# Windowed attention and two MLPs in fp32 on one core: scores on quarters of the array, PSUM banks shared out anew, weight splits moved and joined

## The chip, the cores and the metric

The kernel runs on one core of a Trainium2 chip. The metric is the device time of one execution in microseconds; "before" was measured in three runs. A profile of one execution gives, for each engine, when every instruction began and what it waited for. PE is TensorE's matmul stream and PEld its weight loads, DVE is VectorE, ACT is ScalarE, POOL is GpSimd, SP is SyncE, which issues nearly all DMAs.

## The reference, cut to what matters

```python
# q, k, v: (batch 4, heads 8, seq 576, head_dim 64)
scores = scale * np.matmul(q, k.transpose(0, 1, 3, 2))
mask = (rel >= 0) & (rel < 64)               # rel = query position - key position
attn = softmax(np.where(mask, scores, -1e9)) # with +1e-9 under the division
x = np.matmul(attn, v)                       # laid out as (2304 tokens, 512)
x = square(relu(x @ w_in1)) @ w_out1         # (512, 2048), (2048, 512)
x = elu(x @ w_in2) @ w_out2                  # the same sizes
```

The weights come as 64-bit floats, the rest as fp32.

## The kernel before

**Numbers.** Attention multiplies plain fp32. Everything after it multiplies a high part and a low part of each operand (`split`: ACT makes the high part by a copy, DVE subtracts it from the original), three products in place of one (`mm3`, L468; `prod`, L686; `prod2`, L884). A 64-bit weight is turned into fp32 words by `decode64` (ACT into `top`, DVE into `y`) before it is split.

**Attention.** The 2,304 tokens are cut into blocks of 512, 256, 512, 512 and 512 (t = 0 to 4), and heads go in pairs (p = 0 to 3), so there are 20 units. `u_S` forms the scores (L380). Since a query sees 64 keys back, a group of 64 queries needs 128 keys. The tile `qd` holds, for each group, the queries of both heads of the pair, each head in its own 64 rows and its own 64 columns, and zeros elsewhere; one 128x128 matmul with contraction over 128 rows then gives 64 queries of both heads against 128 keys. A block of 512 takes eight such matmuls, four to a PSUM bank. Of each 128x128 piece DVE adds the mask and takes the maximum, ACT the exponential and the sum; then DVE divides, one instruction for each piece (ACT does it in block 1). `u_T` transposes (L421), `u_PV` multiplies by V (L434): two matmuls for each group, one for each head, which use 64 columns of the array each (128 rows by 64 columns).

**First MLP.** `m_h` (L468, PSUM tile `ph`) and `m_out` (L468, PSUM tiles `o`) run over blocks 0 to 2, with the attention of later blocks between them. Blocks 3 and 4 go together by a scheme with seven products in place of eight (`stepw`, `prod`, L686, with `outw`); its weights are sums and differences of weight quarters, written to DRAM once (`wd0`) and loaded back (`w0_load`, L706).

**Second MLP.** Its weights take the same form: the generator `portions` decodes, sums, splits and stores them (`put`, L243; tensors `wd1`, `wd2` in DRAM), a step at each `slot()` in the main program. There are 16 tasks of seven quarter matrices, so 112 quarters of 256 KB. The second MLP reads the activations back from DRAM (`x2d`, written by `leave1`, L512) into tiles `xq` (`x_read`, L630), makes its operands `xo` of them (`x_make`) and loads weights as `wr` (`unit_load`, L610). The tiles `xq` take over memory in which `leave1` held block 3's outputs, so they come after those stores.

**What sets the order.** A scheduler lays out every engine's instructions before the run; each engine, SP with its DMAs included, then works through its list in order. All vector and scalar instructions go through one helper, so their line is L54: tiles tell them apart.

Of the kernel before, what the change touches and what calls it, by code (L numbers as in the profile page):

```python
# [26 lines left out]
def window_attention_then_two_mlps(  # L27
# [61 lines left out]
    ps_a = pool(ctx, "ps_a", 2, space=PSUM)  # L89
    ps_h = pool(ctx, "ps_h", 2, space=PSUM)  # L90
# [10 lines left out]
    def zero_q(x, eng):  # L101
        for r in range(2):
            eng.memset(x[r * D:(r + 1) * D, :, 1 - r, :], 0.0)

    def zeros():
        for x in qd:
            zero_q(x, vec)

    def constants():
# [11 lines left out]
        nc.gpsimd.memset(mask[1][:, 0:WIN], NEG)  # L121
# [48 lines left out]
    def decode64(y, z, x):  # L170
# [4 lines left out]
        )  # L175
        vec.scalar_tensor_tensor(
            out=y, in0=x.rearrange("p f w -> p (f w)").bitcast(U32).rearrange("p (f w) -> p f w", w=2)[:, :, 0],
            scalar=13, in1=z, op0=ALU.logical_shift_right, op1=ALU.bitwise_or,
        )

    def w_split(u):
# [8 lines left out]
        if LA <= u < LA + 2:  # L190
            for k, (j, i) in enumerate(UNITS[u]):
# [43 lines left out]
    def put(i, p, k, x):  # L235
        o = small([P, 2, HW], "wo")
        if i == 1:
            z = o.rearrange("p y (m a j) -> p y a m j", m=FT, j=TB)
            split(z[:, 0], z[:, 1], x.rearrange("p (a m j) -> p a m j", m=FT, j=TB), vec)
        else:  # L240
            split(o[:, 0], o[:, 1], x, vec)
        d = wd2[k][:, p] if i == 1 else (wd1 if i == 0 else wd0)[p][:, ORD1.index(k)]
        nc.sync.dma_start(out=d, in_=o.bitcast(F32))  # L243
# [903 lines left out]
```

## Time and profile before

| | us |
|---|---|
| median of three runs (lowest, highest) | 851.28 (850.07, 852.8) |
| the profiled execution, and the span that its trace shows | 852.89, 851.1 |
| PE busy in the span | 819.2 (96%) |
| PEld busy | 747.1 (88%) |
| DVE busy, ACT busy | 590.2 (69%), 579.2 (68%) |
| DMA: bytes moved, mean rate | 214.86 MB, 252 GB/s |

A matmul's duration in the trace is longer than its share of the engine, since matmuls overlap: what a matmul costs is the distance from its start to the next start. One fp32 matmul of the attention leaves two records on PE; a product of high and low parts and a transpose leave one.

### The profile page before, as it was taken

What the parts mean: (1) busy time and instruction counts of PE and PEld (TensorE: products, weight loads), DVE (VectorE), ACT (ScalarE), POOL (GpSimd) and SP (SyncE); (2) the same over time, 40 slices, a digit from 0 to 9 for tenths busy, and PEclk for the clock granted to TensorE, in tenths of its full rate; (3) what the DMA queues carried; (4) which work ended last, traced back from release to release, by engine and by line L of the source; (5) the groups of instructions that cost most, each with busy time, mean ns of one, the idle gap of its engine ahead of it and who ended that gap; (6) DMA issues with size and microseconds to landing.
All of it is one profiled execution on the core that took longest, in us unless ns stands there. A gap on an engine that the chain in (4) does not pass through costs nothing.

```text
span 851.1 us, 14626 instructions
## 1 busy us (share of the span) xinstructions
PE 819.2 (96%) x4908; PEld 747.1 (88%) x4908; DVE 590.2 (69%) x1505; ACT 579.2 (68%) x1353; POOL 5.5 (1%) x21
## 2 busy tenths in 40 slices
PE   6799999999999999999999399999999999999998
PEld 5578889998888888888878299999999999999998
DVE  7777416978466777666667456688767799576875
ACT  6899547787677678867765357766577666477652
POOL 2000000000000000000000000000000000000000
PEclk9999999999999999999999699999999999999999
DMA  9997224657266479999789768788987886877842
GB/s 302 371 400 267 89 76 139 199 191 226 84 230 196 155 236 392 362 345 341 266 287 378 247 230 306 278 304 259 276 294 283 300 261 217 276 266 273 308 131 56
DMA packets 120715, 214.86 MB, mean 252 GB/s; under 512 B 46144, under 2 KB 75328, under 8 KB 112192
## 3 DMA queue, kind: packets, MB, share of 16 engines
q1 hardware_dynamic: 119808, 213.73, 73.0%
q8 instruction: 39, 0.64, 0.3%
q14 instruction: 36, 0.29, 0.1%
q10 hardware_dynamic: 832, 0.20, 0.1%
HBM read 160.41 MB, written 53.48 MB: 251 GB/s over the span
## 4 chain that ended last, share of the span: by engine, by line
PE 85%; DMA 5%; DVE 4%; ACT 4%; issue 1%; SPq 0%; ACTq 0%; DVEq 0%
PE o L468 20%; PE po L884 20%; PE px L686 14%; PE ph L468 11%; PE py L686 10%; PE po L686 6%; PE pa L380 2%; DMA wd<-tl 2%; DVE pb L54 1%; PE pa L434 1%; DMA top<-in_moe_w_out_dram 1%; PE pa L421 1%; DVE y L54 1%; PE px L884 1%; ACT top L54 1%
## 5 line engine op out<-in xcount | busy, mean ns | idle before, releaser
L468 PE MATMUL o<-gs,w 128*128 128x512 f32 (+1 forms) x960 | 217.1, 373 | 0.3 <-ACT ev L54 0.3
L468 PEld LDWEIGHTS o<-gs,w 128*128 128x128 f32 x960 | 167.7, 190 | 30.2 <-ACT ev L54 1.1
L884 PE MATMUL po<-g,wr 128*128 128x384 f32 (+1 forms) x972 | 168.6, 333 | 0.0
L884 PEld LDWEIGHTS po<-g,wr 128*128 128x128 f32 x972 | 167.5, 188 | 0.0
L468 PE MATMUL ph<-xs,w 128*128 128x512 f32 (+1 forms) x576 | 130.0, 366 | 5.6 <-ACT xs L54 3.0
L54 ACT ACTIVATE g<-gr 128x384 fp32r<-128x384 f32 x168 | 86.9, 523 | 56.2 <-PE po L884 49.8
L468 PEld LDWEIGHTS ph<-xs,w 128*128 128x128 f32 x576 | 97.1, 193 | 21.7 <-ACT xs L54 4.0
L54 DVE TENSOR_TENSOR g<-gr,g 128x384 fp32r<-128x384 f32 x168 | 89.9, 551 | 16.1 <-ACT g L54 15.1
L686 PE MATMUL px<-xo,wr 128*128 128x384 f32 x432 | 85.3, 338 | 11.8 <-ACT xo L54 11.5
L686 PEld LDWEIGHTS px<-xo,wr 128*128 128x128 f32 x432 | 76.5, 190 | 12.8 <-ACT xo L54 11.9
L54 DVE TENSOR_TENSOR gs<-g,gs 128x512 fp32r<-128x512 f32 (+1 forms) x64 | 39.8, 623 | 48.1 <-ACT gs L54 47.3
L54 ACT ACTIVATE sy<-px 128x384 f32<-128x384 f32 x69 | 33.8, 490 | 42.2 <-PE px L686 41.7
L54 ACT ACTIVATE pb<-pb,nm 128x128 f32<-128x128 f32 x144 | 55.8, 390 | 9.1 <-DVE nm L54 9.0
L686 PE MATMUL py<-xo,wr 128*128 128x384 f32 x288 | 57.2, 339 | 1.3 <-ACT xo L54 0.7
L686 PE MATMUL po<-xo,wr 128*128 128x384 f32 x288 | 56.2, 334 | 0.0
L686 PEld LDWEIGHTS py<-xo,wr 128*128 128x128 f32 x288 | 51.2, 190 | 2.2 <-ACT xo L54 1.2
L54 DVE TENSOR_TENSOR gr<-gr 128x384 f32<-128x384 f32 x96 | 52.1, 552 | 0.5
L54 DVE TENSOR_TENSOR gr<-sy,py 128x384 f32<-128x384 f32 x48 | 26.6, 554 | 35.7 <-PE py L686 23.3
L686 PEld LDWEIGHTS po<-xo,wr 128*128 128x128 f32 x288 | 50.5, 188 | 0.0
L686 PE MATMUL px<-xo,w 128*128 128x512 f32 x192 | 46.5, 389 | 0.0
L54 ACT ACTIVATE g<-ph 128x512 f32<-128x512 f32 (+1 forms) x48 | 24.7, 517 | 29.0 <-PE ph L468 28.8
L686 PEld LDWEIGHTS px<-xo,w 128*128 128x128 f32 x192 | 36.0, 188 | 7.5
(91 smaller groups left out, 1139.5 us busy)
## 6 DMA issues: line engine op xcount, KB each, us to landing
wr<-wd SPq DMA_DIRECT2D x66, 1024.0 KB, 6.4
wr<-wd SPq DMA_DIRECT2D x24, 768.0 KB, 5.3
wd<-tl SPq DMA_DIRECT2D x56, 256.0 KB, 4.1
w<-wd SPq DMA_DIRECT2D x56, 256.0 KB, 4.8
wd<-wo SPq DMA_DIRECT2D x56, 256.0 KB, 4.9
vr<-in_v_dram SPq DMA_DIRECT2D x16, 512.0 KB, 5.2
wd<-xs SPq DMA_DIRECT2D x32, 256.0 KB, 2.6
wraw<-in_moe_w_in_dram SPq DMA_DIRECT2D x16, 511.8 KB, 8.2
```

Of the source, the lines that this page charges most:

```text
L54: r = fn(*a, **kw)
L380: nc.tensor.matmul(out=ps[:, i * P:(i + 1) * P], lhsT=qr[:, b0 + i].rearrange("p a x -> p (a x)"), rhs=kr[:, o:o + P], start=True, stop=True,)
L421: nc.tensor.transpose(out=ps[:, i:i + P], in_=pb[:, i:i + P], identity=ident)
L434: nc.tensor.matmul(out=ps[d, b * WIN:(b + 1) * WIN], lhsT=vr[:, b % 2, b // 2, d], rhs=pt[:, d], start=True, stop=True,)
L468: last["pe"] = nc.tensor.matmul(out=ps, lhsT=a[x], rhs=b[y], start=(first and i == 0), stop=(final and i == 2))
L686: last["pe"] = nc.tensor.matmul(out=ps[:, :NH], lhsT=w[:, wr_, c * P:(c + 1) * P], rhs=x[:, xr_, c], start=first and n == 0, stop=final an ...
L884: last["pe"] = nc.tensor.matmul(out=ps[m][:, lo:hi], lhsT=w[:, y, m * P:(m + 1) * P], rhs=s[:, x, lo:hi], start=k in fresh and p == 0 and ...
```

## The change

It has five parts.

1. **Scores on quarters.** `q` is loaded as it is, by one DMA, without zeros. A matmul now takes 64 rows of one head (`qr[d, ...]`) and 64 queries: a quarter of the array. Four of them (two heads, two groups of 64 queries) do what two matmuls did. Each head has a PSUM bank of its own; a 128x128 piece now holds two groups of one head.
2. **PSUM.** The pools for `ph` and `pa` (two banks each) give way to four banks handed out by `among`: `ph` has two in block 0 and one afterwards; the attention has two, and three from block 1 on.
3. **One division a bank.** One DVE instruction over 512 columns, with the reciprocals broadcast, replaces four, in block 1 too.
4. **High parts of the first MLP's weights on DVE** (`split_v`), not on ACT.
5. **Second layer's parts two at a time.** `put` takes two quarters where they lie side by side, with one split (two in `wd2`) and mostly one DMA; `stage` replaces `small` and hands out buffers of two quarters; the order in `wd1` and `wd2` fits that. The slots are as many as before.

```diff
--- before.py
+++ after.py
@@ -86,25 +86,14 @@
...
     wts = pool(ctx, "wts", 1)
-    ps_a = pool(ctx, "ps_a", 2, space=PSUM)
-    ps_h = pool(ctx, "ps_h", 2, space=PSUM)
     ps_o = pool(ctx, "ps_o", 1, space=PSUM)
...
-    mask = [cst.tile([P, P], F32, name=f"mask{i}") for i in range(2)]
-    qd = [at.tile([P, 2 * NQ, 2, D], F32, tag=f"qd{i}", name=f"qd{i}", bufs=1) for i in range(2)]
+    mask = [cst.tile([P, P], F32, name=f"mask{i}") for i in range(3)]
...
+    def split_v(hi, lo, x):
+        vec.tensor_copy(hi, x)
+        vec.tensor_tensor(out=lo, in0=x, in1=hi.bitcast(F32), op=ALU.subtract)
...
-                split(w[:, 0], w[:, 1], yf[:, k], vec)
+                split_v(w[:, 0], w[:, 1], yf[:, k])
...
-        split(w[:, :, 0, :], w[:, :, 1, :], yf, vec)
+        split_v(w[:, :, 0, :], w[:, :, 1, :], yf)
...
-    ORD1 = ["a11", "a12", "s2", "s1", "s3", "a22", "s4"]
+    ORD1 = ["a11", "a12", "s2", "s1", "s4", "s3", "a22"]
...
+    ORDK = [1, 2, 5, 6, 7, 4, 3]
...
-    wd2 = {n: drp.tile([P, NP, 2, HW], F32, name=f"wd2_{n}") for n in ORD2}
+    wd2 = drp.tile([P, 7, NP, 2, HW], F32, name="wd2")
...
     def put(i, p, k, x):
-        o = small([P, 2, HW], "wo")
+
...
+        m = x.shape[1]
+        hi, lo, o = stage(m)
...
+            d = wd2[:, ORDK.index(k):ORDK.index(k) + m, p]
         else:
...
-        nc.sync.dma_start(out=d, in_=o.bitcast(F32))
...
+            split(hi, lo, x, vec)
+            d = (wd1 if i == 0 else wd0)[p][:, ORD1.index(k):ORD1.index(k) + m]
+        if o is None:
+            for r, z in enumerate((hi, lo)):
+                nc.sync.dma_start(out=d[:, :, r], in_=z.bitcast(F32))
+        else:
+            nc.sync.dma_start(out=d, in_=o.bitcast(F32))
...
+        left, right = yf[:, :, :HW], yf[:, :, HW:]
+
+        def sums(p, i):
+            sub2(q21, q21, q22, ALU.add)
+            sub2(q11, q21, q11)
+            put(i, p, "s2", left)
+            yield
+            sub2(right, right, yf[:, 0:1, :HW].broadcast_to([P, 2, HW]))
+            put(i, p, "s4", right)
+            yield
...
-            sub2(q21, q21, q22, ALU.add)
-            put(2, p, "s1", q21)
-            sub2(q11, q21, q11)
-            put(2, p, "s2", q11)
-            yield
-            sub2(q12, q12, q11)
-            put(2, p, "s4", q12)
-            sub2(q22, q22, q11)
-            put(2, p, "s3", q22)
-            yield
+            yield from sums(p, 2)
...
-                put(i, p, 1, q11)
-                put(i, p, 2, q21)
-                put(i, p, 3, q22)
+                put(i, p, 1, left)
+                put(i, p, 3, yf[:, 1:2, HW:])
                 yield
                 sub2(q12, q12, q11)
-                put(i, p, 5, q12)
                 sub2(q22, q22, q12)
-                put(i, p, 6, q22)
+                put(i, p, 5, right)
                 yield
                 sub2(q11, q22, q11)
-                put(i, p, 7, q11)
                 sub2(q21, q21, q22)
-                put(i, p, 4, q21)
+                put(i, p, 7, left)
...
-                qr = sc.tile([P, 2 * NQ, 2, D], F32, tag="gs", name="qd", bufs=GB)
-                zero_q(qr, nc.gpsimd)
+                qr = sc.tile([P, NMAX], F32, tag="gs", name="qd", bufs=GB)
             else:
...
-                qr = qd[p % 2]
+                qr = at.tile([P, NMAX], F32, tag="qd", name="qd", bufs=2)
...
-            for a in range(2):
...
-                nc.sync.dma_start(
-                    out=qr[w, :2 * m, a, :],
-                    in_=q[p, w, t0:t0 + n].rearrange("d (b x) -> d b x", x=WIN),
-                )
+            nc.sync.dma_start(out=qr[:, :n], in_=q[p, :, t0:t0 + n])
...
     def u_S(u, alloc):
...
         qr, kr = raw[u]["q"], raw[u]["k"]
+        m = BLOCKS[t] // P
...
-        for b0, m in banks(t):
-            ps = alloc()
-            for i in range(m):
-                o = (b0 + i) * WIN
-                nc.tensor.matmul(
-                    out=ps[:, i * P:(i + 1) * P],
-                    lhsT=qr[:, b0 + i].rearrange("p a x -> p (a x)"), rhs=kr[:, o:o + P],
-                    start=True, stop=True,
-                )
+        pss = [alloc() for _ in range(2)]
+        for i in range(m):
+            for a in range(2):
+                d = slice(a * D, (a + 1) * D)
+                for c in range(2):
+                    o = (2 * i + c) * WIN
+                    nc.tensor.matmul(
+                        out=pss[a][c * WIN:(c + 1) * WIN, i * P:(i + 1) * P],
+                        lhsT=qr[d, o:o + WIN], rhs=kr[d, o:o + P], start=True, stop=True,
+                    )
+        prb[u] = []
...
             pb = at.tile([P, 4 * P], F32, tag="pb", name="pb", bufs=4)
...
                 vec.tensor_tensor_reduce(
-                    out=pb[:, c], in0=ps[:, c], in1=mask[(T0[t] + b * WIN) % S == 0],
+                    out=pb[:, c], in0=pss[a][:, z], in1=mask[1 + lead.index(True) if any(lead) else 0],
...
-            r = rc[:, b0:b0 + m]
...
+            r = rc[:, b0:b0 + w]
...
             vec.reciprocal(out=r, in_=r)
...
-            for i in range(m):
-                c, b = slice(i * P, (i + 1) * P), b0 + i
-                if t == 1:
...
-                    act.activation(
...
-                    )
...
-                    continue
-                last["dve"] = vec.tensor_scalar(
-                    out=pb[:, c], in0=pb[:, c], scalar1=rc[:, b:b + 1], scalar2=None, op0=ALU.mult
-                )
-            prb[u, b0] = pb
...
+            last["dve"] = vec.tensor_tensor(
+                out=x, in0=x, in1=r.unsqueeze(2).broadcast_to([P, w, P]), op=ALU.mult
+            )
+            prb[u].append((pb, w))
...
-        for b0, m in banks(u[0]):
-            pb = prb.pop((u, b0))
+        for pb, w in prb.pop(u):
...
-        for b, pt in enumerate(pts):
+        m = BLOCKS[t] // P
+        for b in range(2 * m):
             for a in range(2):
...
-                    out=ps[d, b * WIN:(b + 1) * WIN],
-                    lhsT=vr[:, b % 2, b // 2, d], rhs=pt[:, d], start=True, stop=True,
+                    out=ps[d, b * WIN:(b + 1) * WIN], lhsT=vr[:, b % 2, b // 2, d],
+                    rhs=pts[a * m + b // 2][:, (b % 2) * WIN:(b % 2 + 1) * WIN], start=True, stop=True,
...
-        ps = ps_h.tile([P, 512], F32, tag="h", name="ph")
+        ps = h_alloc(t)
...
-    a_alloc = lambda: ps_a.tile([P, 512], F32, tag="a", name="pa")
...
+    def spot(k, name):
+        return ps_o.tile([P, 512], F32, tag=f"b{k}", name=name)
...
+    def among(ks, name):
+        turns[ks] = turns.get(ks, -1) + 1
+        return spot(ks[turns[ks] % len(ks)], name)
+
+    def h_alloc(t):
+        return among((0, 1) if t == 0 else (0,), "ph")
+
+    def a_alloc():
+        return among((1, 2, 3) if late[0] else (2, 3), "pa")
...
-    def small(shape, name):
-        turn[1] += 1
-        if la:
-            return la[0].tile(shape, F32R, tag=f"gs{turn[1] % 4}", name=name, bufs=1)
-        if lw and turn[1] % 6 < 4:
-            return lw[0].tile(shape, F32R, tag="wo", name=name, bufs=4)
-        if hw:
-            return half(2 + turn[1] % 2)
-        return xs[1, turn[1] % KD][:, :, HW:]
...
+    def stage(m):
+
+        n = turn[1] = turn[1] + 1
+        if lw or hw:
+            if n % 3 == 0 and hw:
+                o = hw[1].rearrange("p y f -> p (y f)").rearrange("p (k y f) -> p k y f", k=2, y=2)
+            elif lw:
+                o = lw[0].tile([P, 2, 2, HW], F32R, tag="wo", name="wo", bufs=2)
+            else:
+                o = at.tile([P, 2, 2, HW], F32R, tag="wo", name="wo", bufs=1)
+            o = o[:, :m]
+            return o[:, :, 0], o[:, :, 1], o
+        if n % 3 == 0:
+            o = at.tile([P, 2, 2, HW], F32R, tag="wo", name="wo", bufs=1)[:, :m]
+            return o[:, :, 0], o[:, :, 1], o
+        k = 2 * (n % 3) - 2
+        return *(xs[1, (k + r) % KD][:, :m, HW:] for r in range(2)), None
...
-        src = wd1[p] if kind == "p" else wd2[p]
+        src = wd1[p] if kind == "p" else wd2[:, ORDK.index(p)]
...
-            return ps_h.tile([P, 512], F32, tag="h", name="px")
+            return among((0, 1), "px")
...
-            return ps_a.tile([P, 512], F32, tag="a", name="py")
+            return among((2, 3), "py")
...
+        if (t, j) == (1, 0):
+            late[0] = 1
```

**PE, first MLP of block 1 (`ph`, `o` 128x256) with the scores of block 2 between (`pa<-kr,qd`).** Before:

```order
L468 MATMUL ph<-xs,w 128x256 x12
L380 MATMUL pa<-kr,qd_90 128x128 x8
L468 MATMUL o_1496<-gs,w 128x256 x3
L468 MATMUL o_1497<-gs,w 128x256 x3
L468 MATMUL o_1498<-gs,w 128x256 x3
L468 MATMUL o_1499<-gs,w 128x256 x3
```

After the change, at the same place:

```order
L454 MATMUL ph<-xs,w 128x256 x12
L366 MATMUL pa<-kr,qd 64x128 x2
L454 MATMUL o_1500<-gs,w 128x256 x3
L454 MATMUL o_1501<-gs,w 128x256 x3
L454 MATMUL o_1502<-gs,w 128x256 x3
L454 MATMUL o_1503<-gs,w 128x256 x3
L366 MATMUL pa<-kr,qd 64x128 x7
L454 MATMUL ph<-xs,w 128x256 x12
L366 MATMUL pa<-kr,qd 64x128 x9
```

Eight scores in one piece have become sixteen quarters in two pieces, of seven and nine; the two ahead of them end the unit before. In blocks 1 to 4 PE's list holds 112 score matmuls before and 224 after. Count as a visit every stretch in which PE uses part of the array (quarters, or V's halves) between matmuls on the whole array: 9 visits before, all of V, and 44 after.

**SP, from the stores of block 3's outputs (`x2d`) to the first read for the second MLP (`xq`).** Before, the last eleven rows:

```order
L166 DMA top<-in_moe_w_out_dram 128x1023
L610 DMA wr<-wd_2_99 128x2048
L243 DMA wd_1_113<-wo 128x512
L243 DMA wd_2_114<-wo 128x512
L610 DMA wr<-wd_2_99 128x1536
L243 DMA wd_3_119<-wo 128x512
L243 DMA wd_5_116<-wo 128x512
L243 DMA wd_6_115<-tl 128x512
L243 DMA wd_7_117<-tl 128x512
L243 DMA wd_4_118<-wo 128x512
L630 DMA xq<-x2d_91 128x2x384
```

After the change, the whole stretch:

```order
L498 DMA x2d_87<-ev 128x512 x4
L248 DMA wd_106<-tl 128x2x512
L248 DMA wd_106<-wo 128x2x512
L160 DMA top<-in_moe_w_out_dram 128x1023
L616 DMA wr<-wd_0_90 128x2048
L248 DMA wd_106<-wo 128x2x512
L248 DMA wd_106<-tl 128x512
L616 DMA wr<-wd_0_90 128x1536
L248 DMA wd_106<-wo 128x2x512 x2
L616 DMA wr<-wd_1_91 128x2048
L636 DMA xq<-x2d_84 128x2x384
```

Before, 35 DMAs stand between the last `x2d` store of block 3 and the first `xq`: 21 quarters to store, 8 loads of raw weights, 6 loads `wr`. After, there are 10: 6 stores with 11 quarters, 1 load, 3 loads `wr`. At the first `w0_load` 24 quarters have been stored in SP's list before and 30 after, at block 2's first `x2d` store 25 and 38.

## Rows read from the trace of the kernel before

**Rows 1.** Stretches: start:end, length, busy of each engine, PEclk, DMA share, GB/s.

```profile
20.00:44.00 24.00, 17.47 (x154) 11.94 (x152) 19.09 (x53) 20.45 (x42) 0.00 (x0) 0.93 0.98 370
44.00:314.00 270.00, 268.99 (x1899) 234.82 (x1900) 175.67 (x605) 197.27 (x531) 0.00 (x0) 0.99 0.57 188
314.00:422.00 108.00, 108.00 (x478) 89.19 (x477) 74.20 (x164) 85.39 (x188) 0.00 (x0) 1.00 0.96 346
471.00:492.00 21.00, 7.95 (x21) 5.73 (x20) 12.26 (x21) 8.57 (x15) 0.00 (x0) 0.60 0.60 210
492.00:786.00 294.00, 294.00 (x1688) 292.70 (x1687) 215.46 (x411) 194.50 (x402) 0.00 (x0) 1.00 0.80 275
```

**Rows 2.** Waits from 418 to 500 us: who waited for whom, total, times, longest.

```profile
PE px L686 <- ACT xo L54: 11.5, 1, 11.5
ACT xo L54 <- DMA xq<-x2d: 8.8, 2, 7.5
```

**Rows 3.** SP's queue in order of time: start, length, DMA.

```profile
438.69 1.02 SPq L512 DMA_DIRECT2D x2d<-ev  x1
...
475.35 0.68 SPq L243 DMA_DIRECT2D wd<-wo  x1
476.09 3.36 SPq L630 DMA_DIRECT2D xq<-x2d  x6
```

**Rows 4.** PE and ACT in order of time, 469 to 489 us.

```profile
469.76 1.75 PE L468 MATMUL o<-gs,w 128*128 128x512 f32 x7
...
482.08 0.84 ACT L54 ACTIVATE xo<-xq 128x768 fp32r<-128x768 f32 x1 [7.49 <-DMA xq<-x2d]
...
482.98 0.69 PE L686 MATMUL px<-xo,wr 128*128 128x384 f32 x1 [11.47 <-ACT xo L54]
...
487.90 1.97 PE L686 MATMUL py<-xo,wr 128*128 128x384 f32 x5 [0.58 <-DVE xo L54]
```

**Rows 5.** PE in order of time around one piece of scores and one of V.

```profile
149.78 1.95 PE L380 MATMUL pa<-kr,qd 128*128 128x128 f32 x16
151.48 1.68 PE L468 MATMUL o<-gs,w 128*128 128x256 f32 x12
153.00 1.60 PE L468 MATMUL ph<-xs,w 128*128 128x256 f32 x12
154.44 1.60 PE L468 MATMUL o<-gs,w 128*128 128x256 f32 x12
...
163.36 1.36 PE L468 MATMUL ph<-xs,w 128*128 128x256 f32 x10
164.65 2.09 PE L434 MATMUL pa<-pt,vr 128*64 128x64 f32 x64
166.67 0.50 PE L468 MATMUL ph<-xs,w 128*128 128x256 f32 x2
167.01 1.60 PE L468 MATMUL o<-gs,w 128*128 128x256 f32 x12
168.44 0.88 PE L468 MATMUL ph<-xs,w 128*128 128x256 f32 x6
```

**Rows 6.** The same V piece in two short windows: merged records begun so far.

```profile
164.65 0.34 PE L434 MATMUL pa<-pt,vr 128*64 128x64 f32 x4
164.65 0.45 PE L434 MATMUL pa<-pt,vr 128*64 128x64 f32 x8
```

**Rows 7.** Groups up to 45 us, one PE wait there, and the page's group of `ph`'s first reader.

```profile
L54 ACT ACTIVATE w<-y 128x512 fp32r<-128x512 f32 x6 | 3.6, 625 | 2.2 <-DVE y L54 2.2
L54 ACT ACTIVATE w<-y 128x1024 fp32r<-128x1024 f32 x2 | 2.1, 1056 | 2.1 <-DVE y L54 2.1
L54 DVE TENSOR_TENSOR w<-y,w 128x1024 fp32r<-128x1024 f32 x2 | 2.5, 1225 | 2.2 <-ACT w L54 2.2
...
44.16 6.20 PE L468 MATMUL ph<-xs,w 128*128 128x512 f32 x19 [1.82 <-ACT g L54]
...
L54 ACT ACTIVATE g<-ph 128x512 f32<-128x512 f32 (+1 forms) x48 | 24.7, 517 | 29.0 <-PE ph L468 28.8
```

More of the change, by code (lines that the diff above doesn't have):

```diff
@@ L120, in constants @@
                 )
-        nc.gpsimd.memset(mask[1][:, 0:WIN], NEG)
+        for i in range(2):
+            nc.gpsimd.memset(mask[1 + i][i * WIN:(i + 1) * WIN, 0:WIN], NEG)
         make_identity(nc, ident)
@@ L235, in put @@
     def put(i, p, k, x):
-        o = small([P, 2, HW], "wo")
+        m = x.shape[1]
+        hi, lo, o = stage(m)
         if i == 1:
-            z = o.rearrange("p y (m a j) -> p y a m j", m=FT, j=TB)
-            split(z[:, 0], z[:, 1], x.rearrange("p (a m j) -> p a m j", m=FT, j=TB), vec)
-        else:
-            split(o[:, 0], o[:, 1], x, vec)
-        d = wd2[k][:, p] if i == 1 else (wd1 if i == 0 else wd0)[p][:, ORD1.index(k)]
-        nc.sync.dma_start(out=d, in_=o.bitcast(F32))
+            for n in range(m):
+                split(
+                    *(z[:, n].rearrange("p (m a j) -> p a m j", m=FT, j=TB) for z in (hi, lo)),
+                    x[:, n].rearrange("p (a m j) -> p a m j", m=FT, j=TB), vec,
+                )
+            d = wd2[:, ORDK.index(k):ORDK.index(k) + m, p]
+        else:
+            split(hi, lo, x, vec)
[5 more added lines that the diff above has]
+            nc.sync.dma_start(out=d, in_=o.bitcast(F32))
     def portions():
@@ L363, in u_load @@
             nc.sync.dma_start(out=vr[:, :, :m, :], in_=v[p, :, :, c0:c0 + m, :])
-    def banks(t):
-        nb = BLOCKS[t] // WIN
-        return [(b, min(4, nb - b)) for b in range(0, nb, 4)]
     def u_S(u, alloc):
@@ L375, in u_S @@
         rc = at.tile([P, 2 * NQ], F32, tag="rc", name="rc")
[L376 to L387 removed]
+        pss = [alloc() for _ in range(2)]
[9 more added lines that the diff above has]
+        prb[u] = []
+        for a0, heads in ((0, 1), (1, 1)) if m == NQ else ((0, 2),):
+            w = heads * m
+            pb = at.tile([P, 4 * P], F32, tag="pb", name="pb", bufs=4)
+            for i in range(w):
+                a, g = a0 + i // m, i % m
+                b = a * m + g
+                c, z = slice(i * P, (i + 1) * P), slice(g * P, (g + 1) * P)
+                lead = [(T0[t] + (2 * g + h) * WIN) % S == 0 for h in range(2)]
                 vec.tensor_tensor_reduce(
[L389 removed]
+                    out=pb[:, c], in0=pss[a][:, z], in1=mask[1 + lead.index(True) if any(lead) else 0],
                     scale=-SCALE, scalar=3.0e38, op0=ALU.add, op1=ALU.min,
@@ L396, in u_S @@
                 )
-            r = rc[:, b0:b0 + m]
+            b0 = a0 * m
+            r = rc[:, b0:b0 + w]
             vec.tensor_scalar(
-                out=r, in0=sm[:, b0:b0 + m], scalar1=1.0e-9, scalar2=None, op0=ALU.add
+                out=r, in0=sm[:, b0:b0 + w], scalar1=1.0e-9, scalar2=None, op0=ALU.add
             )
             vec.reciprocal(out=r, in_=r)
-            for i in range(m):
-                c, b = slice(i * P, (i + 1) * P), b0 + i
-                if t == 1:
-                    act.activation(
-                        out=pb[:, c], in_=pb[:, c], func=AF.Copy, scale=rc[:, b:b + 1]
-                    )
-                    continue
-                last["dve"] = vec.tensor_scalar(
-                    out=pb[:, c], in0=pb[:, c], scalar1=rc[:, b:b + 1], scalar2=None, op0=ALU.mult
-                )
-            prb[u, b0] = pb
+            x = pb[:, :w * P].rearrange("p (b x) -> p b x", x=P)
+            last["dve"] = vec.tensor_tensor(
+                out=x, in0=x, in1=r.unsqueeze(2).broadcast_to([P, w, P]), op=ALU.mult
+            )
+            prb[u].append((pb, w))
     def u_T(u, alloc):
         pts = []
-        for b0, m in banks(u[0]):
-            pb = prb.pop((u, b0))
+        for pb, w in prb.pop(u):
             ps = alloc()
-            for i in range(0, m * P, P):
+            for i in range(0, w * P, P):
                 nc.tensor.transpose(out=ps[:, i:i + P], in_=pb[:, i:i + P], identity=ident)
             pt = at.tile([P, 512], F32, tag="pt", name="pt", bufs=4)
-            copy(pt[:, :m * P], ps[:, :m * P], act)
-            pts += [pt[:, i:i + P] for i in range(0, m * P, P)]
+            copy(pt[:, :w * P], ps[:, :w * P], act)
+            pts += [pt[:, i:i + P] for i in range(0, w * P, P)]
         return pts
@@ L537, in decode @@
                 wd[0] += 1
-    a_alloc = lambda: ps_a.tile([P, 512], F32, tag="a", name="pa")
+    def spot(k, name):
+        return ps_o.tile([P, 512], F32, tag=f"b{k}", name=name)
     rot = [0]
+    turns = {}
+    def among(ks, name):
[5 more added lines that the diff above has]
+        return among((1, 2, 3) if late[0] else (2, 3), "pa")
+    late = [0]
     def o_alloc():
```

30 lines of the change are left out of this document (5 added, 25 removed).

## The prediction

> **What bounds the kernel now.** I read the stretches first, since one busy share over 851 us mixes stages with different limits. PE is busy for 269 of 270 us from 44 to 314, for all of 314 to 422 and for all of 492 to 786 [rows 1]: there only less PE work, or a stall that is added, can move the time. It loses time in two places.
>
> The first is the start, up to 44 us, where block 0's attention and the decoding of the first weights go through ACT and DVE. From 20 to 44 us PE is busy for 17.5 of 24 us, ACT for 20.5 and DVE for 19.1 [rows 1]: both are nearly full, and ACT is the fuller. PE's last wait there, 1.82 us, is for ACT [rows 7].
>
> The second is the step into the second MLP, 471 to 492 us. PE starts 21 matmuls there, with a mean granted clock of 0.60 [rows 1]. At full clock, 12 of 384 columns at 0.174 us (294 us by 1688) and nine of 512 at 0.226 (108 us by 478) [rows 1] are 4.1 us of work, so 16.9 of the 21 us are lost, the slow clock after the idle time included. The waits say why: PE waits 11.5 us for ACT's `xo`, and ACT waits for the DMA `xq` [rows 2]. `xq` is issued at 476.09, right behind a store of the second layer's prepared quarters at 475.35 [rows 3]. ACT starts on the first operand 6.0 us after that issue, and PE starts with the second 11.8 us after it (482.08 and 487.90) [rows 4]. PE's queue of `o` matmuls ends at about 471.5 [rows 4].
>
> **The change, part by part.**
>
> *Scores.* PE is the bound where the scores of blocks 1 to 4 stand, so this part counts in full. Before: 112 matmuls, two records each. In the piece at 149.78, 16 records and 12 `o` matmuls take 3.22 us to 153.00; 12 matmuls take 1.44 (153.00 to 154.44), which leaves 1.78, so 0.111 a record and no cost for entering or leaving the piece [rows 5]. All 224 records: 25 us.
>
> After: 224 quarters, 448 records of the same 128 columns. No row shows such a quarter. The nearest is V, which uses half of the array's columns: 4 records last 0.34 [rows 6] and 64 of them 2.09 [rows 5], so 60 take 1.75, or 0.029 each. They have 64 columns where a score's record has 128, so one at a time they would need half of 0.111, 0.056: the two halves of the columns work at the same time. If the two halves of the rows do so as well, a quarter's record takes 0.111 / 4 = 0.028. If not, 0.056; if none overlaps, 0.111. For the 448 records that is 12.5, 25 or 50 us. I take 12.5, because two halves overlap completely where a row shows them and the order issues the four quarters of a set next to each other; 25 and 50 stay as rivals.
>
> V also shows a cost that full-array scores lack. From 163.36 to 168.44 us there are 5.08 us with 24 `ph` and `o` matmuls (10, 2 and 12, at 0.120: 2.88) and 64 V records at 0.029 (1.86) [rows 5]. That leaves 0.34 for going onto a part of the array and back. The Trainium skill, in "TensorEngine Tiling (Array Packing)", section "Key Properties", says that changing the tiling mode drains TensorE; that speaks against this change, and the row's 0.34 us agrees. The order counts 9 visits before and 44 after, so 35 x 0.34 = 11.9 us, and I add 0.7 for sets of four that are cut and for scores right beside V. Saved 12.5, paid 12.6: **0**, with -1 to +2 for a record between 0.026 and 0.032. What the new scores gain in the array goes to the visits. By the same page and section, different tiles can run matmuls in parallel, which would be the 12.5 taken above; no row here shows it for rows of the array.
>
> *Second layer's parts two at a time, and `xq`.* The work of preparing is the same in bytes, but it comes earlier in the order against the main program. Between block 3's last `x2d` store, issued at 438.69, and `xq` at 476.09 [rows 3] there were 21 quarters in 37.4 us, 1.78 us each; now there are 11. At that pace `xq` is issued 19.6 us after the store, at about 458.5. PE needs the first operand at 471.5, so an issue by 471.5 - 6.9 = 464.6 (6.9 is from 476.09 to PE's start at 482.98 [rows 4]). The second operand is needed about 2.5 us later: issue by 471.5 + 2.5 - 11.8 = 462.2. Margin: 4 us. Then PE doesn't stop, so its clock doesn't fall either. I take **-16** of the 16.9, since the first operands come by pieces; bounds 0 (late as before) and -17. The work that hides the earlier preparation is PE's matmuls: in 44 to 314 us DVE has 94 of 270 us free, ACT 73, and the DMA share is 0.57 [rows 1].
>
> *High parts of the first MLP's weights on DVE.* Up to 44 us ACT gives up 3.6 + 2.1 = 5.7 us [rows 7]. DVE takes on the same 5,120 columns. No row shows DVE making this copy; at the price of its subtraction, 1225 ns for 1024 columns [rows 7], it is 6.1 us, which would bring DVE from 19.1 to about 25 of 24 us, less what the joined divisions save; at nothing, ACT's 5.7 are gained. So -5.7 to +1. I take **-2**, nearer to the dear end: the row is for the same columns on the same engine, but a hand-over between engines goes, a `q` tile comes with one DMA in place of two, and the memsets of `qd` fall out. In a sentence of its own: the Trainium skill, "VectorE: DVE Perf Modes", "Mode 2×_2P", lets a single-source fp32 copy in SBUF run at two elements a cycle, which would make the copy about 3 us (an estimate from that page) and the sum some 2 us lower; no run here shows it.
>
> *One bank for `ph` after block 0.* The next `ph` waits for ACT's Relu on the one before. That Relu takes 0.517 us and spends 28.8 of 29.0 idle us waiting for PE, so it comes promptly [rows 7]; the twelve `o` matmuls between two `ph` last 1.44 us [rows 5] at 256 columns, more at 512. **+1**; 0 if it is always prompt, +4 if at one `ph` in four of the 32 ACT is in another instruction of the attention first, and the Relu ends 0.5 later than the cover reaches. Where it is late, PE's whole queue stands behind `ph`.
>
> *One division a bank, `split_v` after 44 us, three `pa` banks:* nothing on the path, as DVE and ACT have the free time just named; without that cover the moved copies cost what the row above says, 1.2 us for 1024 columns.
>
> **Sum.** 852.9 (the profiled execution) + 0 - 16 - 2 + 1 = 835.9. That execution was 1.6 above the median of the three runs, so **834** in their terms. Its own range, by the bounds above: 827 to 841.
>
> **Rivals.**
>
> 1. *Rows of the array don't overlap* (a record takes 0.056). For it: V's rows show halves of the columns only, and all V matmuls use the 128 rows. Against it: nothing in the trace. The scores then cost 25 + 12.6 where they cost 25, so +12.6: **847**. Still faster than before.
> 2. *`xq` is as late as before.* The stores stand earlier in the order, but SP works in order, and each store waits for ACT, DVE and a raw load. If ACT and DVE make the quarters no sooner, the queue arrives at `xq` as late. For it: ACT is busy 85 and DVE 74 of 108 us from 314 to 422, and the DMA share is 0.96 [rows 1]. Against it: the free time in 44 to 314. 834 + 16: **850**, no change.
> 3. *Slower: quarters run one at a time.* A record takes 0.111, the scores 50 us + 12.6: +37.6, so **872**. For it: nothing but that a quarter was never seen; against it: V's halves. All else brings -17, so the change gains nothing from the point where the records cost 25 + 17 - 12.6 = 29.4 us, 0.066 us each.
> 4. *Slower: first-layer weights of blocks 3 and 4 come late.* `w0_load` stands in SP's list behind 30 stored quarters instead of 24, and at block 2's first `x2d` store it is 38 instead of 25. If the 13 more fall into 314 to 422, where DMA has nothing free, each brings 0.26 MB to store and 0.30 MB to load (a task's 2.1 MB of raw words over seven quarters), 1.6 us at 346 GB/s [rows 1]: 21 us of PE waiting for `w`. Then 834 + 21: **855**. It decides when more than about 11 of the 13 fall there; in the trace of before the room is ahead of 314.
>
> **Chances.** Forecast 0.53 (834), rival 1 0.24 (847), rival 2 0.10 (850), rival 3 0.05 (872), rival 4 0.08 (855). A difference under 0.3%, 2.6 us, is about what a measurement here can't tell from none: faster is below 848.7, slower above 853.8. The forecast and nearly all of rival 1 are faster, some of rival 2 also: 0.77. Same: most of rival 2 and a little of rivals 1 and 4, 0.10. Slower: rival 3 and most of rival 4, 0.13. The range reaches from the forecast's lower bound, 826, over rivals 1 and 2 to 852 and leaves out rivals 3 and 4.
>
> **What would show it.** Scores: 16 quarters in a piece at about 0.9 us of records and 0.3 of change, so a piece plus its twelve matmuls about as long as before; at 0.056 a record a block of 512 columns shows PE busy but 0.9 us longer for each unit. `xq`: issued near 458 on the clock of before, no PE wait for `xo`, a granted clock of 1.0 through the step. Start: first `ph` of the long busy stretch some 2 us earlier, DVE fuller than ACT. `ph`: PE waits for ACT `g` of about 1 us in sum. Wrong it would be above all by the pitch of a quarter, which no row shows, and by when the quarters are ready, which the order doesn't tell.

## The result

| | before | after |
|---|---|---|
| median of four runs (lowest, highest), us | 851.6 (850.07, 852.8) | 838.84 (837.73, 840.44) |
| the profiled execution, and its span | 852.89, 851.1 | 837.73, 836.0 |
| PE busy in the span | 819.2 | 816.8 |

The ratio is 0.9853, 95% interval 0.9828 to 0.9877: 12.8 us faster, 17.3 were forecast.

The same stretches as [rows 1], and for the step into the second MLP the two that now hold it. Columns as there.

```profile
20.00:44.00 24.00, 20.39 (x188) 14.58 (x181) 21.41 (x61) 19.39 (x53) 0.00 (x0) 0.86 1.03 417
44.00:314.00 270.00, 268.78 (x2088) 224.15 (x2087) 188.31 (x519) 180.87 (x474) 0.00 (x0) 1.00 0.58 201
314.00:422.00 108.00, 108.00 (x478) 89.43 (x477) 70.93 (x151) 83.49 (x180) 0.00 (x0) 1.00 0.94 338
455.00:476.00 21.00, 21.00 (x97) 17.77 (x96) 13.29 (x17) 10.35 (x16) 0.00 (x0) 1.00 0.84 295
476.00:490.00 14.00, 14.00 (x71) 12.51 (x70) 5.95 (x11) 4.96 (x10) 0.00 (x0) 1.00 0.65 204
```

The hole of [rows 1] at 471 to 492 us is gone: PE is busy throughout, at a granted clock of 1.00. SP's queue from the last stores of block 3's outputs on, to compare with [rows 3]:

```profile
438.04 2.17 SPq L498 DMA_DIRECT2D x2d<-ev  x4
440.30 0.41 SPq L248 DMA_DIRECT2D wd<-tl  x1
...
450.14 4.49 SPq L248 DMA_DIRECT2D wd<-wo  x2
454.72 0.42 SPq L616 DMA_DIRECT2D wr<-wd  x1
455.19 4.95 SPq L636 DMA_DIRECT2D xq<-x2d  x6
```

`xq` is issued at 455.2, 20.9 us sooner. In all fourteen kernels measured here the stores of all 144 quarters stand ahead of `xq` in SP's list, and `xq` is issued at most 5.5 us after DVE has made the last quarter (475.1 and 476.1 before, 454.2 and 455.2 after). So `xq` comes early when the preparation ends early. PE meets no wait for `xo` ([rows 4] for before):

```profile
454.74 18.98 PE L454 MATMUL o<-gs,w 128*128 128x512 f32 x83
473.55 1.23 PE L692 MATMUL px<-xo,wr 128*128 128x384 f32 x6
474.62 1.20 PE L692 MATMUL py<-xo,wr 128*128 128x384 f32 x6
```

**Where the time went.** Counting the MLPs' matmuls and comparing when the same one in the count starts gives the account. The 361st (before block 2's attention): 130.6 before, 127.6 after, so 3.0 us won at the start. The 1,201st (blocks 3 and 4 have begun, the attention is over): 326.3 and 328.8, so 5.5 us lost between. The 1,921st (in the second MLP): 505.4 and 490.3, so 17.6 won at the step. The sum, 15.1, is the difference of the two spans. The medians differ by 12.8, since the profiled execution before is as slow as the slowest of its four and the one after the fastest of its four; so each of these terms is known to 2 or 3 us at best.

4.6 of the 5.5 us lost show in PE's small pieces. I took each distance from a start to the next and subtracted a full MLP matmul's own 0.120 or 0.227. From 44 to 316 us the scores take 24.3 us before and 26.5 after, V 16.6 and 19.9, the transposes 13.2 and 13.8, and waits between MLP matmuls 2.3 and 0.8.

Two pieces of scores of the changed kernel in PE's order of time:

```profile
199.78 1.00 PE L454 MATMUL o<-gs,w 128*128 128x256 f32 x7
200.71 1.10 PE L366 MATMUL pa<-kr,qd 64*64 64x128 f32 x32
201.74 0.74 PE L454 MATMUL o<-gs,w 128*128 128x256 f32 x4
...
219.73 0.63 PE L454 MATMUL o<-gs,w 128*128 128x512 f32 x2
220.29 1.09 PE L366 MATMUL pa<-kr,qd 64*64 64x128 f32 x16
221.31 1.65 PE L454 MATMUL o<-gs,w 128*128 128x512 f32 x6
```

32 records take 1.03 us from their start to the next MLP matmul's, and 16 take 1.02. In the first piece the records begin in fours, 0.109 us from one four to the next: all four quarters of the array work at once, a fourth of a full-array record's 0.111 each. In the second they begin in twos, again 0.109 apart: PE's order has only one head's two quarters there, and half of the rows idle. That the other head's bank was not free yet when the order was laid out is my reading. From 40 to 320 us, 436 records need 109 steps of four; there are 167 steps, 56 of four, 95 of two and 16 others.

### The profile page after: what moved, and what is told of

Read it like the earlier page. It is cut to its first block, busy times and chain, and to the rows that moved or that the text cites. A ratio compares the mean times of both kernels' runs of the same rounds, so it can differ in the third digit from the quotient of the medians.

```text
span 836.0 us, 14761 instructions
## 1 busy us (share of the span) xinstructions
PE 816.8 (98%) x5196; PEld 734.7 (88%) x5196; DVE 590.6 (71%) x1372; ACT 553.0 (66%) x1278; POOL 5.0 (1%) x23
## 4 chain that ended last, share of the span: by engine, by line
PE 91%; ACT 5%; DMA 2%; DVE 1%; issue 1%; SPq 0%; ACTq 0%
PE o L454 23%; PE po L890 20%; PE px L692 14%; PE ph L454 12%; PE py L692 10%; PE po L692 6%; ACT pb L54 3%; PE pa L420 2%; PE pa L366 2%; PE pa L406 1%; PE px L890 1%; DMA tl<-in_moe_w_in_dram 1%; DMA wd<-wo 0%; DMA wraw<-in_moe_w_in_dram 0%; ACT top L54 0%
## 5 line engine op out<-in xcount | busy, mean ns | idle before, releaser
L454 PE MATMUL ph<-xs,w 128*128 128x512 f32 (+1 forms) x576 | 126.0, 362 | 1.9 <-ACT xs L54 1.7
L454 PEld LDWEIGHTS ph<-xs,w 128*128 128x128 f32 x576 | 94.9, 189 | 19.2 <-ACT xs L54 2.6
L54 DVE TENSOR_TENSOR g<-gr,g 128x384 fp32r<-128x384 f32 x168 | 89.9, 552 | 16.1 <-ACT g L54 15.1
L54 DVE TENSOR_TENSOR wo<-y,wo 128x256 fp32r<-128x256 f32 (+1 forms) x65 | 32.2, 508 | 19.3 <-ACT wo L54 18.5
```

The costliest lines, as they stand in the source:

```text
L54: r = fn(*a, **kw)
L454: last["pe"] = nc.tensor.matmul(out=ps, lhsT=a[x], rhs=b[y], start=(first and i == 0), stop=(final and i == 2))
```

## The experiments

All times are medians, and differences between the starts of the same MLP matmul are between profiled executions, on each one's own clock; each run's ratio stands beside runs of the kernel before on the same chip. Three numbers of each trace tell the story. "Last V" is the start of the last V matmul, the end of the attention. "Prepared" counts quarters whose low part DVE has begun by 320 us, of 144, 32 sums for the first layer included (the lead named in the expectations is counted so).

| run | us | ratio (95%) | last V | prepared | `xq` issued |
|---|---|---|---|---|---|
| before | 851.6 | | 307.9 | 58 | 476.1 |
| the change | 838.84 | 0.9853 (0.9828 to 0.9877) | 283.7 | 72 | 455.2 |
| pairs_alone | 854.25 | 1.0030 (1.0014 to 1.0046) | 306.7 | 58 | 479.2 |
| quarters_single | 845.42 | 0.9923 (0.9897 to 0.9949) | 292.5 | 67 | 459.1 |
| banks_undone | 864.29 | 1.0143 (1.0117 to 1.0168) | 307.9 | 58 | 485.8 |
| banks_alone | 848.77 | 0.9956 (0.9942 to 0.9969) | 288.3 | 67 | 463.3 |
| two_pa | 863.93 | 1.0147 (1.0122 to 1.0172) | 308.8 | 58 | 483.6 |
| whole | 850.71 | 0.9992 (0.9979 to 1.0005) | 289.4 | 67 | 472.2 |
| apart | 852.55 | 1.0007 (0.9995 to 1.0019) | 291.5 | 67 | 473.9 |
| full_array | 838.43 | 0.9838 (0.9809 to 0.9867) | 278.1 | 69 | 458.5 |
| high_on_act | 846.22 | 0.9941 (0.9926 to 0.9956) | 291.7 | 67 | 463.2 |
| banks_div_high | 839.59 | 0.9855 (0.9833 to 0.9877) | 279.9 | 72 | 453.5 |
| full_late | 837.19 | 0.9834 (0.9807 to 0.9860) | 276.1 | 72 | 455.3 |
| full_shared | 838.74 | 0.9848 (0.9832 to 0.9865) | 282.8 | 69 | 464.3 |

### Is it the parts two at a time that bring `xq` forward?

**quarters_single** puts `put`, `portions` and the buffers of before back into the changed kernel:

```diff
-        m = x.shape[1]
-        hi, lo, o = stage(m)
+        o = small([P, 2, HW], "wo")
```

> The changed kernel with the second layer's parts prepared one quarter at a time again, in the slots and the order of the kernel before. Theory (the gain of 17.5 us at the step into the second MLP comes from this part alone): xq is issued near 475 us again, PE idles some 11 us there and its clock falls, about 16 us more than the changed kernel, 855, slower than the kernel before. Rival (the gain comes with the other parts, which free ACT and SP earlier): 839 to 843.

Measured 845.42, and `xq` at 459.1: early, with quarters one at a time. The theory fell. The 6.6 us more than the changed kernel lie elsewhere: the same MLP matmul starts within 0.4 us of the changed kernel's up to the 841st, 7.6 us later at the 1,201st and 8.1 in the second MLP.

**pairs_alone** is the other half: the kernel before with part 5 and nothing else (its buffers of two quarters are `tl`'s memory, `xs`, and `wo` in the pool `lw`).

```diff
-        o = small([P, 2, HW], "wo")
+        m = x.shape[1]
+        hi, lo, o = stage(m)
...
-                put(i, p, "a11", q11)
-                put(i, p, "a12", q12)
+                put(i, p, "a11", yf[:, 0].rearrange("p (k f) -> p k f", k=2))
```

> The kernel before with the second layer's parts two at a time and nothing else (with other buffers for them, since memory has no room for one of them). Theory: the step into the second MLP loses its 17 us and nothing else changes, 834 to 836, a little faster than the changed kernel, since the scores cost it 2 to 5 us. Rival (the other parts are needed too): between 840 and 851.

Measured 854.25, slower than before by 0.3%, and `xq` at 479.2. PE's waits from 420 to 520 us, as in [rows 2]:

```profile
PE px L686 <- ACT xo L54: 14.7, 1, 14.7
```

Part 5 gives none of the 17.6 us. It does bring stores forward in SP's list: 27 DMAs stand between the last `x2d` store and `xq`, and before 35. But DVE makes the last quarter at 478.7, no sooner than before, and `xq` waits for that.

### The banks

The second theory is read from SP's order: with the new banks, and only with them, the preparation's stores stand early against those of `x2d`.

**banks_undone** gives `ph` and `pa` two banks each in the changed kernel:

```diff
-        return among((0, 1) if t == 0 else (0,), "ph")
+        return among((0, 1), "ph")
...
-        return among((1, 2, 3) if late[0] else (2, 3), "pa")
+        return among((2, 3), "pa")
```

> The changed kernel with the banks as before: two for ph, two for pa, throughout. New theory (the banks, by letting the attention run ahead, give the second layer's preparation its lead of 14 quarters at 320 us, and so the early xq): the lead goes, xq is issued after 470 us, PE waits 5 to 11 us for xo, 849 to 853. Rival (the parts two at a time and the freed engines give the lead): xq near 456, 838 to 840.

Measured 864.29: `xq` as late as forecast, at 485.8, and a loss that the theory did not name. PE's waits from 40 to 520 us:

```profile
PE px L692 <- DMA w<-wd: 20.1, 1, 20.1
PE px L692 <- ACT xo L54: 6.3, 1, 6.3
```

The first is for the first-layer weights of blocks 3 and 4: the prediction's rival 4, in another kernel and by another road, as the next run but one shows. The loss was outside the forecast of 849 to 853.

**banks_alone** is the kernel before with the four banks (`spot`, `among`, `h_alloc`, `a_alloc`, `late`) and nothing else.

```diff
-        ps = ps_h.tile([P, 512], F32, tag="h", name="ph")
+        ps = h_alloc(t)
...
-    a_alloc = lambda: ps_a.tile([P, 512], F32, tag="a", name="pa")
+    def a_alloc():
+        return among((1, 2, 3) if late[0] else (2, 3), "pa")
```

> The kernel before with the four banks of the changed one and nothing else. New theory: 66 to 70 quarters by 320 us in place of 58, xq issued by 462 us, no wait for it, so 17 us less at that step; some of it may go again between 250 and 310 us, as in the run with single quarters (8 us there): 834 to 843. Rival: 850 to 852, xq near 475.

Measured 848.77. From the 1,201st MLP matmul to the 1,921st it goes from 14.0 us behind the kernel before to 3.8 ahead: 17.7 us won at the step by the banks alone, the whole of that gain. The stretch of [rows 1], 471 to 492 us, in this run:

```profile
471.00:492.00 21.00, 21.00 (x99) 18.07 (x99) 15.57 (x21) 11.21 (x18) 0.00 (x0) 1.00 0.56 195
```

The time is still outside the 834 to 843 forecast, since the attention costs more: PE's waits between MLP matmuls grow from 2.3 to 5.5, the transposes with their waits from 13.2 to 17.2, V from 16.6 to 21.6, in 23 pieces in place of 9.

**two_pa** keeps `ph` on one bank and gives `pa` two; the fourth bank lies idle.

```diff
-        return among((1, 2, 3) if late[0] else (2, 3), "pa")
+        return among((2, 3), "pa")
```

> The changed kernel with ph on one bank after block 0, as there, but pa on two banks throughout: one bank lies idle. Theory (the third pa bank gives the preparation its lead): about 58 quarters by 320 us, xq after 475 us, 850 to 864 as with the banks undone. Rival (the single ph bank does it, by shifting the order): 72 quarters by 320 us, xq near 456, 838 to 842.

Measured 863.93 with 58 quarters by 320 us: it is the third `pa` bank. SP's queue in order of time shows where the wait for `w` comes from:

```profile
300.16 0.33 SPq L248 DMA_DIRECT2D wd<-tl  x1
317.38 0.33 SPq L248 DMA_DIRECT2D wd<-wo  x1
319.89 0.32 SPq L498 DMA_DIRECT2D x2d<-ev  x1
...
326.88 3.27 SPq L712 DMA_DIRECT2D w<-wd  x4
```

and its waits from 295 to 330 us what it stood for:

```profile
SPq L248 <- DVE wo L54: 17.7, 2, 16.8
```

SP waits 16.8 us for a prepared quarter, and the loads `w`, which the order has behind 30 stored quarters (24 in the kernel before), come 28 us after those of the changed kernel (299.0). PE then waits 11.3 us for them. DVE in order of time shows why that quarter is late:

```profile
303.04 0.69 DVE L54 TENSOR_TENSOR gs<-g,gs 128x512 fp32r<-128x512 f32 x1 [2.91 <-ACT gs L54]
309.11 0.69 DVE L54 COPY xr<-pa 128x512 f32<-128x512 f32 x1 [5.38 <-PE pa L420]
...
315.52 1.22 DVE L54 TENSOR_TENSOR xo<-xr,xo 128x1024 fp32r<-128x1024 f32 x1
316.66 0.69 DVE L54 TENSOR_TENSOR wo<-y,wo 128x512 fp32r<-128x512 f32 x1
```

DVE stands 5.38 us waiting for PE's last V, then works mostly on that output (`xr`) and the operands made of it (`xo`), and only then makes the quarter. So it is the late end of the attention that reaches the preparation here. pairs_alone, where the attention ends as late, has 24 quarters ahead of `w` and no such wait.

In the changed kernel and all seven runs with three `pa` banks and early `xq`, V ends at 276 to 293 us; in the four kernels with two, at 307 to 309. At the start of the last V, 51 to 56 of the 144 quarters are begun in every one of the fourteen kernels, 56 in nine of them; from 340 us on every kernel takes 1.8 to 1.9 us a quarter. So the time at which the attention ends goes most of the way to say when `xq` comes. The pace turns there: before, 5 quarters in each of 280 to 300 and 300 to 320 us, then 11 in 320 to 340; after, 10, 9 and 11. The attention's memory is then handed to buffers of the preparation: with single quarters their first store is at 324.9 us before, at 305.3 in banks_alone and 294.9 in banks_div_high. That the memory, and not only the freed time of DVE and ACT, sets the pace is argued; no run separates the two.

### The quarters of the array

**whole** lets each unit's first quarter write the bank that comes free last, with the others held behind it, so that sets of four stay together:

```diff
-            for a in range(2):
+            for a in (1, 0):
...
+                    with ExitStack() as line:
+                        for ins in held_by:
+                            line.enter_context(tc.issue_after(ins.ins))
...
+                    held_by = held_by or [mm]
```

> The changed kernel with the first score matmul of each unit writing the bank that comes free last and the others held behind it, so that sets of four stay together. Theory (sets of four run at once, but the order of the changed kernel often issues only one head's two quarters at a time): from 40 us on 61 of 167 steps of 0.109 us go, so 5 to 6.6 us less than the changed kernel, 832 to 834. Rival (the cost is in the visits, each with its 0.34, not in the steps): only two or three visits fewer, under 1 us, 838.

The sets came together: 98 steps of four, 30 others. The scores take 24.1 us from 44 to 316, 2.4 less than in the changed kernel, with a wait of 1.1 for a bank in them. By the steps it would be 4.2 (39 x 0.109), so the theory is borne out in sign; of the 5 to 6.6 forecast it shows 2.4, or 3.5 without that wait. The run is slower all the same, 850.71: at the 1,201st MLP matmul it is 0.4 us ahead of the changed kernel, in the second MLP 13.0 behind, since `xq` comes at 472.2 and PE waits for it:

```profile
PE px L697 <- ACT xo L54: 6.1, 1, 6.1
```

It has three `pa` banks and an attention that ends early, at 289.4, with 56 quarters begun, and its preparation still falls behind: 76 by 340 us, where high_on_act, whose attention ends later, has 79. So the third bank is needed for the lead but doesn't secure it; what slows the preparation between 290 and 340 us here is open.

**apart** puts all of one head ahead of all of the other.

```diff
-            for a in (1, 0):
-                d = slice(a * D, (a + 1) * D)
+        for a in (1, 0):
+            d = slice(a * D, (a + 1) * D)
+            for i in range(m):
...
-                    held_by = held_by or [mm]
+                    held_by = [mm]
```

> The changed kernel with all quarters of one head ahead of all of the other, so that only the two halves of the columns are in use at a time. Theory (halves of the rows overlap when a set is together): 224 steps in place of the 167 plus block 0's, about 5 us more than the changed kernel, 843 to 845. Rival (halves of the rows never overlap): no change, 839.

Measured 852.55. Its `xq` is as late as that of whole, so it is to be compared with that run: the same number of pieces, 166 steps of two against 10, the scores 27.7 us against 24.1. The order costs 3.6 us in blocks 1 to 4 and 1.8 in the median. Two pieces of this run and the same two of whole:

```profile
100.80 0.68 PE L370 MATMUL pa<-kr,qd 64*64 64x128 f32 x16
...
201.08 1.59 PE L370 MATMUL pa<-kr,qd 64*64 64x128 f32 x32
202.60 0.50 PE L459 MATMUL o<-gs,w 128*128 128x256 f32 x2
```

```profile
100.40 0.67 PE L370 MATMUL pa<-kr,qd 64*64 64x128 f32 x16
...
198.48 1.10 PE L370 MATMUL pa<-kr,qd 64*64 64x128 f32 x32
199.51 0.50 PE L459 MATMUL o<-gs,w 128*128 128x256 f32 x2
```

The expectation that only halves of the columns would be in use did not come true. Sixteen records take as long in either order. Of 32, one head's sixteen begin while eight of the other's have still to start: 12 steps in 1.52 us, against 8 in 1.03; one head after the other would take 16. So the rows overlap, wholly or in part, where both heads stand in one piece, and the 3.6 us are only a part of what that overlap is worth.

**full_array** leaves only the quarters out: `q` between zeros as before, all the rest of the change but one buffer, for which memory has no room. Against the changed kernel:

```diff
-                        out=pss[a][c * WIN:(c + 1) * WIN, i * P:(i + 1) * P],
-                        lhsT=qr[d, o:o + WIN], rhs=kr[d, o:o + P], start=True, stop=True,
+                    out=ps[:, i * P:(i + 1) * P],
+                    lhsT=qr[:, b0 + i].rearrange("p a x -> p (a x)"), rhs=kr[:, o:o + P],
```

> All of the change but the quarters of the array: scores on the full array, with q between zeros, and for want of room one staging buffer less. Theory (scores and V pieces in the changed kernel cost PE 5 to 6 us more than before between 44 and 316 us, since sets are broken and V is cut into more visits): 832 to 835. Rival (quarters pay for themselves): 838 to 845. If xq comes late for the missing buffer: 849.

Measured 838.43 against 838.84, intervals overlapping: the quarters are worth nothing that can be measured. They don't reach 832 to 835 without them either, since the full-array scores also come in more pieces (31 for 25, 25.4 us) and V in 17.

### The start

**high_on_act** undoes part 4.

```diff
-                split_v(w[:, 0], w[:, 1], yf[:, k])
+                split(w[:, 0], w[:, 1], yf[:, k], vec)
...
-        split_v(w[:, :, 0, :], w[:, :, 1, :], yf)
+        split(w[:, :, 0, :], w[:, :, 1, :], yf, vec)
```

> The changed kernel with the high parts of the first MLP's weights on ScalarE again. Theory (part 4 gives most of the 2.9 us at the start): the long busy stretch begins 2 to 3 us later, 841 to 842. Rival (the start is set by block 0's attention): 838 to 839.

Measured 846.22, 7.4 more, beyond what either expectation had. The 361st MLP matmul starts 7.2 us later than in the changed kernel. The work up to 46 us in the changed kernel, by line and form, to be held against [rows 7]:

```profile
L54 DVE CAST w<-y 128x512 fp32r<-128x512 f32 x6 | 2.4, 423 | 0.1
L54 DVE CAST w<-y 128x1024 fp32r<-128x1024 f32 x2 | 1.4, 689 | 0.0
```

DVE copies 1,024 columns in 689 ns where ACT took 1056 and DVE's subtraction 1225, and the idle times ahead of the subtraction, 2.2 + 1.6 us before, most of them for ACT, are gone. In this run they are 1.2 + 1.6. The granted clock differs as well, 0.85 from 0 to 20 us against 1.00 in the changed kernel; what that adds to the 7.2 us is not separated.

**banks_div_high** is banks_alone with one division a bank (part 3) and `split_v` (part 4): full-array scores, single quarters. Against banks_alone:

```diff
+            last["dve"] = vec.tensor_tensor(
+                out=x, in0=x, in1=r.unsqueeze(2).broadcast_to([P, m, P]), op=ALU.mult
+            )
...
-        split(w[:, :, 0, :], w[:, :, 1, :], yf, vec)
+        split_v(w[:, :, 0, :], w[:, :, 1, :], yf)
```

> The kernel before with the four banks, one division a bank and the high parts on VectorE; full-array scores and single quarters stay. New theory: as with the banks alone, and 1 to 3 us less at the start and for the attention: 832 to 841. Rival: 848 to 851.

Measured 839.59, 9.2 less than banks_alone. Between the two profiles it is 5.5 us by the 361st MLP matmul (6.7 ahead of before where banks_alone is 1.2 ahead) and 10.2 by the 1,201st, so the rest comes in the attention. Parts 2, 3 and 4 alone make the whole gain.

### Versions of it

**full_late** is full_array with the third `pa` bank from block 2 on, not from block 1.

```diff
-        return among((0, 1) if t == 0 else (0,), "ph")
+        return among((0, 1) if t < 2 else (0,), "ph")
...
-        if (t, j) == (1, 0):
+        if (t, j) == (2, 0):
             late[0] = 1
```

> The run with full-array scores, with the third pa bank (and so the single ph bank) from block 2 on and not from block 1. Theory (the lead comes from the third bank while block 2 runs and the attention of blocks 3 and 4 beside it; in block 1 the single ph bank and the finer pieces only cost): xq as early, and 1 to 4 us off the stretch of block 1: 834 to 838. Rival (the bank is needed from block 1 on): xq after 470, 846 to 852.

Measured 837.19. `xq` is as early, so the third bank is needed only from block 2 on. The gain of 1.2 us on full_array is less than either interval.

**full_shared** gives `ph` two banks throughout, of which `pa` uses one as its third.

```diff
-        return among((0, 1) if t == 0 else (0,), "ph")
+        return among((0, 1), "ph")
```

> The run with full-array scores, with ph on two banks throughout and pa on three after block 0, one bank serving both in turn. Theory: the lead stays, since pa has three banks; fewer waits of ph for its reader, 0 to 3 us less, 835 to 839. Rival (a bank that is shared makes ph wait for the attention's readers): 840 to 850.

Measured 838.74, no difference from full_array. Its profile also shows how far one execution can go at the start: PE has the same order as in full_array up to 128 us, and yet the 361st MLP matmul starts 3.5 us later, after raw weights (`wraw`) for which ACT waits 6.8 us in place of 4.8. None of these beats the changed kernel by more than the measurement resolves.

## Why the prediction was right, point by point

The time lay in the range and 4.8 us above the value. That the sum held is partly luck: its one large term had the right size under a wrong cause, and the misses of the small terms, 5.5 lost where 0 and 1 were forecast and 3.0 won where 2 was, stayed small beside it.

1. **`xq`, -16: the size was right (-17.6), the cause was not.** The step that failed stands under "Second layer's parts two at a time, and `xq`": "The work of preparing is the same in bytes, but it comes earlier in the order against the main program." It gave the lead to part 5. I read the place of 11 quarters in SP's order and put it down to the edit that touches those stores. pairs_alone and quarters_single show that part 5 neither makes the lead nor is needed for it; banks_alone, banks_undone and two_pa show that the third `pa` bank makes it. The prediction put that bank under "nothing on the path". Its rival 2 had the right reason, that the stores stand earlier in the order but the quarters are made no sooner: that is what pairs_alone shows.
2. **Scores, 0: measured +2.2 in blocks 1 to 4, and V +3.3.** The quarter's pitch was right: four at once, 0.109 us a step, so rival 1 is out. The visit's cost was right too: 32 records in 1.22 us beyond the MLP matmuls' own time are 8 steps of 0.109 and 0.35. There are 45 pieces of scores and V from 44 to 316 us (44 were counted). What failed is "the order issues the four quarters of a set next to each other": 58 of 167 steps are too many, 6.3 us (the expectation for whole has 61, from too few records). V's nine more pieces are in the 11.9 that the forecast paid for visits.
3. **High parts on DVE, -2: mis-sized.** The copy was priced at 1225 ns for 1024 columns; it takes 689. The Trainium skill, in "VectorE: DVE Perf Modes", "Mode 2×_2P", has such a copy at two elements a cycle, from which the prediction estimated about 3 us for all of them. They took 2.4 + 1.4; from 512 to 1,024 columns the copy grows by 266 ns and the subtraction by 536, so row and page agree on twice the rate, and the dear end of the bounds was the wrong one to lean on. Undoing the part costs 7.4 us, not 2. At the start as a whole only 3.0 appear. full_array, without the quarters, is 6.2 ahead of before at the 361st MLP matmul; that the quarters take the difference back is not shown, since full_shared, with the same start in PE's order, is only 2.7 ahead.
4. **`ph` on one bank, +1: measured the other way.** The wait of 1.82 us in [rows 7] is gone, and of PE's waits from 44 to 320 us two are left, none of them of `ph`:

```profile
PE o L454 <- ACT gs L54: 0.7, 1, 0.7
PE pa L420 <- ACT pt L54: 0.5, 1, 0.5
```

5. **Rival 4** did not happen in the changed kernel (first `w` load at 299.0 us, no wait), but it is real: 20.1 and 11.3 us in the two runs that have 30 quarters ahead of `w` and an attention that ends late.

With the sizes measured the sum reads 852.9 - 3.0 + 5.5 - 17.6 = 837.8, which is no test of them, since they are differences of the two profiles. The forecast's own range of 827 to 841 (826 in the paragraph on chances) is not what its bounds add up to: they give 827.6 to 842 with `xq` at -16, and up to 858 with `xq` at 0.

## What to carry to other kernels

When a queue's order has moved, ask what moved it before giving the gain to the edit that stands nearest: leave that edit out alone, and put it in alone. A third buffer between two engines can end one stage earlier and so hand its memory and its engines to work that only looks unrelated. Quarters of the array overlap in their rows only where work for both halves stands in one piece of PE's order; a bank for each head lets the heads drift apart. Here broken sets and visits cost about as much as the quarters save: the scores take 26.5 us, 24.1 with whole sets, and 24.3 on the full array.

## What was not expected

A low clock cost little at the start. The changed kernel's granted clock is 0.86 from 20 to 44 us, and 0.93 before. In two_pa, with the same work there, it is 1.00, and the 361st MLP matmul starts only 0.5 us sooner. PE in order of time in the changed kernel:

```profile
22.05 0.50 PE L454 MATMUL ph<-xs,w 128*128 128x512 f32 x1 [1.67 <-ACT xs L54]
23.31 1.11 PE L406 MATMUL pa<-ident,pb 128*128 128x128 f32 x4 [0.76 <-DVE xs L54]
...
25.21 2.50 PE L420 MATMUL pa<-pt,vr 128*64 128x64 f32 x32
...
32.29 1.15 PE L420 MATMUL pa<-pt,vr 128*64 128x64 f32 x30
...
101.76 0.67 PE L366 MATMUL pa<-kr,qd 64*64 64x128 f32 x16
102.36 0.73 PE L454 MATMUL o<-gs,w 128*128 128x512 f32 x2
```

32 records of V take 2.50 us at 25.2, after PE had idled 1.67 and 0.76 us, and 30 take 1.15 at 32.3: the lower of the two levels and the upper. The last two rows show how a visit's cost appears: 16 records in four steps of 0.109, 0.44 us, take 0.60 from start to start, and the rest of the 0.35 stands ahead of the first record and behind the matmul that follows.
